# A Fourier filter with a gated convolution: the first batch loaded in 52-row transfers, its first rows sent ahead, and the inverse matrices read from memory

## The chip, the cores and the metric

One Trainium2 chip; the program runs on one of its cores. A core has a matrix engine (TensorE, PE in the profile; PEld is its weight load, which runs beside it), VectorE (DVE), ScalarE (ACT), GpSimd (POOL) and SyncE (SP), which here only issues transfers. Transfers run on 16 DMA engines and are issued from the queues of SP and ACT. PE multiplies out of SBUF (128 partitions) into PSUM; DVE and ACT bring results from PSUM to SBUF. The metric is the time of one launch on the device, in microseconds (us).

## The reference

`x` is 8 batches of 3200 positions with 256 channels. A real Fourier transform along the positions, a complex 256x256 matrix with a bias and a soft threshold on each frequency, the inverse transform; then a gate from a five-tap causal convolution per channel, a value matrix, and an output matrix. Everything is float32.

```python
X = np.fft.rfft(x, axis=1)
Yr = Xr @ w_r - Xi @ w_i + b_r
Yi = Xr @ w_i + Xi @ w_r + b_i
Yr = np.sign(Yr) * np.maximum(np.abs(Yr) - lam, 0.0)      # the same for Yi
x = np.fft.irfft(Y, n=3200, axis=1)
gate = sigmoid(sum(conv_w[k] * shifted(x, k) for k in range(5)))
out = (gate * (x @ w_val)) @ w_out
```

## The kernel before

**The transform in two steps.** 3200 = 50 x 64. A position is n*64 + h*32 + m, with n from 0 to 49, h the half (0 or 1) and m from 0 to 31. Stage 1 (`p1`) transforms over n with the 50x50 matrix `f1`: 50 rows of `x` lie on partitions for each half h (half 1 begins at partition 64), and 50 rows come out, f = 0 to 49, which are the real and imaginary parts of 25 frequency tiles. A batch is cut into 8 units `u` of four m each; one unit is two transfers of 50 rows x 4 KB, four matmuls of 512 columns, a copy out of PSUM, and the stores to a scratch tensor in DRAM, `a_dram`, whose rows are ordered (f, h, m). Stage 2 reads `a_dram` back with the rows on partitions in another arrangement: a frequency tile t is 128 consecutive rows, which come from two values of f. So no tile can be loaded before all 8 units have stored their part of its rows.

**The spectral part** (`p2`) takes two tiles at a time, a pair `u` = 0 to 12 (the last has one tile). Load of `a` (256 KB a pair), stage 2 (`s` in the profile, line 590: f2 matrices), splits into high and low parts on ACT and DVE, the complex matrix in three real products (`k_ps`, line 665, six matmuls; `y_ps`, line 660, twelve), bias, soft threshold (`yb`, `tp`), and, for two pairs at a time, the first inverse stage (`z_ps`, line 703), copied and stored to a second scratch tensor, `z_dram`. The last tile alone ends in line 695, once per batch.

**The last part** (`positions`, `gated`) loads `zl` from `z_dram`, does the second inverse stage (`y_p`, line 759) into `y_sb`, the taps on DVE (line 813), the sigmoid on ACT, the value matmuls `v_ps`, the product with the gate (line 855) and the output matmuls `o_ps` (lines 787 and 791).

**What sets the order.** Nothing is written in engine order. Each piece of work is added to a `Plan` with a priority `at`, an engine, an estimated length, the keys that it reads and writes, and the buffers that it opens. `Plan.order` then plays the program through with these estimates: on each engine, of the pieces that could begin about first, it takes the one with the lowest `at`, and the pieces are emitted in that order. The table `O` shifts the priorities of kinds of work; `SWITCH` is the estimated cost of going between tiled matmuls (mode "q") and others; `WIRE` and `BACKLOG` are a model of the transfers. So a change of any number can move instructions everywhere. Waits on other engines and on transfers are put in by the framework; transfers share eight completion semaphores in turn, so that a queue waits with a ninth until the first has landed.

**The start.** The sixteen transfers of batch 0's `x` go half from SP, half from ACT's queue. PE does warm-up matmuls on a buffer of zeros (line 907) between the units' products (line 508). `f2` is loaded in four parts (pair 0; 1 to 3; 4 to 7; the rest). The matrices of the first inverse stage, `g1`, are the transposes of f2 scaled by 1/64: `make_g1` multiplies f2 with a unit matrix on PE (line 424) and scales on ACT (line 426), pair by pair during batch 0; only the last tile's is loaded. `w_val`, `w_out` and `conv_w` come as float64 words and are converted by 13 operations each on DVE (`from_float64`).

## Time and profile before

| | |
|---|---|
| launch times, 3 runs | 899.44, 899.5 and 904.92 us, median 899.5 |
| span of the profiled execution (first to last instruction) | 897.1 us; the page prints no time of its own for that launch, and the median of the three lies 2.4 us above its span |
| busy: PE, DVE, ACT | 865.2, 763.5, 603.7 us |
| mean granted PE clock | 0.986 |
| data moved | 162.26 MB, 181 GB/s over the span |

In the profile a row of the timeline has start, length, engine, line, operation with output<-input, count, and in brackets the idle time before it with what ended it. In rows of windows each engine has its busy time and, in brackets, its instructions; then the granted PE clock (1.00 is full), the busy share of the 16 DMA engines, and GB/s. PE's float32 matmuls show two records each, so that `x8` of line 590 are four matmuls. Names are without buffer numbers. SPq and ACTq are the engines' issuing of transfers.

### The profile page before, as it was taken

Reading aid. Unit: us, or ns where it says so; the run is one execution under the profiler, and the core shown is the slowest. Engines: PE = TensorE matmul, PEld = TensorE weight load, DVE = VectorE, ACT = ScalarE, POOL = GpSimd, SP = SyncE. Lnnn points to the kernel's source line nnn. Section 1 sums busy time; section 2 is a strip of 40 time slices with the busy share of each in tenths; the row PEclk is TensorE's granted clock in tenths of the full one; section 3 lists DMA queues with packets and bytes.
Section 4 is the critical chain, followed back from the end, with each engine's and each line's share of the span. In section 5 each row is a group of like instructions: output and inputs, shape, how many; then the busy total and the mean of one; then the engine's idle time right before and its main releaser. Section 6 shows DMA issues by size and latency. Waiting matters only on the chain.

```text
span 897.1 us, 24381 instructions
## 1 busy us (share of the span) xinstructions
PE 865.2 (96%) x10370; PEld 741.1 (83%) x10370; DVE 763.5 (85%) x1139; ACT 603.7 (67%) x924; POOL 4.4 (0%) x11
## 2 busy tenths in 40 slices
...
GB/s 203 198 233 239 228 227 217 210 130 182 236 180 179 159 229 218 190 183 160 217 235 158 163 204 217 222 131 174 215 223 154 139 172 109 178 62 116 180 75 91
DMA packets 103439, 162.26 MB, mean 181 GB/s; under 512 B 9154, under 2 KB 77636, under 8 KB 103332
## 3 DMA queue, kind: packets, MB, share of 16 engines
...
## 4 chain that ended last, share of the span: by engine, by line
PE 83%; DVE 10%; DMA 4%; ACT 2%; issue 1%; ACTq 1%; SPq 0%
PE y_ps L660 14%; PE o_ps L791 13%; PE v_ps L791 12%; PE s L590 10%; PE z_ps L703 9%; PE k_ps L665 8%; PE y_p L759 7%; PE p L543 6%; DVE acc L813 4%; DMA x<-in_x 1%; PE v_ps L787 1%; DVE acc L855 1%; DVE gated L317 1%; DMA f_sb<-in_f 1%; DMA a_dram<-s 1%
## 5 line engine op out<-in xcount | busy, mean ns | idle before, releaser
L813 DVE SCALAR_TENSOR_TENSOR acc<-y_sb,cw_sb,acc 128x800 f32<-128x800 f32 (+1 forms) x264 | 255.9, 1018 | 17.6 <-ACT acc L810 17.2
L660 PE MATMUL y_ps<-w_sb,xs 128*128 128x256 f32 x1152 | 155.4, 284 | 0.6 <-DVE xs L648 0.6
L791 PE MATMUL o_ps<-gated,wo_sb 128*128 128x400 f32 x756 | 155.2, 351 | 0.6 <-DVE acc L855 0.6
L660 PEld LDWEIGHTS y_ps<-w_sb,xs 128*128 128x128 f32 x1152 | 144.5, 189 | 11.3 <-DVE xs L652 3.2
L791 PEld LDWEIGHTS o_ps<-gated,wo_sb 128*128 128x128 f32 x756 | 133.5, 188 | 3.1 <-DVE acc L855 0.8
L791 PE MATMUL v_ps<-y_hl,wv_sb 128*128 128x400 f32 x660 | 131.3, 346 | 0.5 <-ACT o L879 0.5
L590 PE MATMUL s<-f_sb,a 128*128 128x128 f32 x800 | 113.2, 284 | 8.2 <-ACT wo_sb L315 3.4
L791 PEld LDWEIGHTS v_ps<-y_hl,wv_sb 128*128 128x128 f32 x660 | 118.5, 188 | 1.6 <-ACT o L879 0.9
L590 PEld LDWEIGHTS s<-f_sb,a 128*128 128x128 f32 x800 | 101.7, 196 | 20.8 <-issue 6.9
L678 ACT ACTIVATE tp<-yb,nlam 128x512 f32<-128x512 f32 (+1 forms) x104 | 73.7, 708 | 38.7 <-DVE yb L674 38.6
L665 PEld LDWEIGHTS k_ps<-w_sb,xs 128*128 128x128 f32 x576 | 77.2, 190 | 20.8 <-issue 10.5
L703 PE MATMUL z_ps<-tp,g_sb 64*64 64x256 f32 x1536 | 93.4, 381 | 0.0
L665 PE MATMUL k_ps<-w_sb,xs 128*128 128x256 f32 x576 | 91.1, 294 | 1.2 <-DVE yb L671 0.9
L759 PEld LDWEIGHTS y_p<-g_sb,zl 50*64 50x64 f32 x4096 | 68.3, 135 | 18.1 <-issue 7.3
L315 ACT CAST gated<-acc 128x800 fp32r<-128x800 f32 x63 | 54.3, 862 | 38.2 <-DVE acc L855 38.0
L759 PE MATMUL y_p<-g_sb,zl 50*64 50x50 f32 x4096 | 72.5, 219 | 7.1 <-issue 4.2
L680 DVE SCALAR_TENSOR_TENSOR tp<-yb,tp 128x512 f32<-128x512 f32 (+1 forms) x104 | 70.0, 673 | 10.6 <-ACT tp L678 10.5
L671 DVE TENSOR_TENSOR yb<-k_ps,bias_sb 128x512 f32<-128x512 f32 x96 | 65.6, 684 | 15.7 <-PE k_ps L665 15.6
L703 PEld LDWEIGHTS z_ps<-tp,g_sb 64*64 64x64 f32 x1536 | 55.3, 133 | 27.4 <-issue 5.1
L855 DVE TENSOR_TENSOR acc<-v_ps,acc 128x800 f32<-128x800 f32 x64 | 62.9, 984 | 16.1 <-PE v_ps L791 12.7
L674 DVE TENSOR_TENSOR yb<-y_ps,yb 128x512 f32<-128x512 f32 x96 | 65.5, 683 | 7.4 <-PE y_ps L660 6.9
L714 ACT COPY z_t<-z_ps 128x1024 f32<-128x1024 f32 x48 | 48.5, 1010 | 25.7 <-PE z_ps L703 25.1
...
## 6 DMA issues: line engine op xcount, KB each, us to landing
zl<-z_dram SPq DMA_DIRECT2D x128, 200.0 KB
...
x<-in_x SPq DMA_DIRECT2D x120, 200.0 KB
a_dram<-s SPq DMA_DIRECT2D x120, 200.0 KB
...
```

What stands on the lines that cost most here:

```text
L590: nc.tensor.matmul(spec()[:, c, :, i, :], tl[ka][:, i, c * P:(c + 1) * P], f2_of(i), start=True, stop=True)
L660: nc.tensor.matmul(p[:, 1 - r, :], xm(hx, c, r), w_sb[:, m, hw, c, :], start=k == 0, stop=k == 5)
L665: nc.tensor.matmul(p, sm(hx, c), w_sb[:, 0, hw, c, :], start=k == 0, stop=k == 5)
L671: nc.vector.tensor_tensor(out=buffer(kb, "yb", [P, 2, D]), in0=tl[kk].rearrange("p (a d) -> p a d", a=1).to_broadcast([P, 2, D]), in1=bias ...
L674: add(at + 0.2, "DVE", dve(2 * D), lambda: nc.vector.tensor_tensor(out=yb(), in0=tl[ky], in1=yb(), op=ALU.add), [ky + (0,)], [kb + (0,)])
L678: nc.scalar.activation(out=buffer(kt, "tp", [P, 2, D])[:, 0:n], in_=tl[kb][:, 0:n], func=AF.Relu, bias=nlam)
L680: add(at + 0.2, "DVE", dve(n * D), lambda: nc.vector.scalar_tensor_tensor(out=tl[kt][:, 0:n], in0=tl[kb][:, 0:n], scalar=LAM, in1=tl[kt][: ...
L703: nc.tensor.matmul(p[e * HP:(e + 1) * HP, i, j * D:(j + 1) * D], g[i * HP:(i + 1) * HP, r, e * HP:(e + 1) * HP], tl[kts[j]][i * HP:(i + 1) ...
L759: nc.tensor.matmul(pv[h][e * HP:(e + 1) * HP, c, m, :], zt[half(h), m, c * P + e * HP:c * P + (e + 1) * HP], g2_sb[half(h), :], start=True ...
L791: nc.tensor.matmul(p[:, e, 0:TB], w[:, hw, c, e * P:(e + 1) * P], src(hy, c), start=n == 0, stop=n == 5)
L813: nc.vector.scalar_tensor_tensor(out=acc(c), in0=y_of(c, j), scalar=cw_sb[:, c, j:j + 1], in1=acc(c), op0=ALU.mult, op1=ALU.add)
L855: add(at + O["gate"], "DVE", dve(2 * TB), lambda: nc.vector.tensor_tensor(out=gate(), in0=hn(tl[kv][:, :, 0:TB]), in1=gate(), op=ALU.mult) ...
```

## The change

**Wider transfers.** `x` is read in 52 rows a half instead of 50 (`NF = N2 + 2`; the two extra rows belong to the next batch and are not multiplied; batch 7 stays at 50), and `a_dram` has 104 rows instead of 100, stored from 52 partitions; rows 50 and 51 of f hold zeros and are read by nobody.

**Batch 0.** Each of the 8 units is its own piece: two transfers (three of the sixteen on ACT's queue, the others on SP's), four matmuls, a copy shared by DVE and ACT. The input lands in the space of `y_sb`, unit 7 in an `x` buffer. Each unit's result is stored in two groups: rows f = 0 to 15 (all that pairs 0 to 3 need) at once, in two transfers of 64 KB, and rows 16 to 51 later, in two of 144 KB. The loads of pairs 0 to 3 wait for the first group alone. The loads of batch 1's `x` come behind pair 3.

**The inverse matrices.** `g1` is computed on the host and loaded in three parts (512, 512 and 576 KB); the transposes, their scalings and the unit matrix are gone. In the first inverse stage one matmul with 64x128 weights takes the place of two with 64x64.

**The order.** The planner now knows the eight semaphores (`LANES`), the supply of PE's instructions in packets (`supplied`), other costs, and table `O` has other values.

```diff
-WARM = 2, 1, 1, 1, 10
+WARM = 6, 1, 1, 1, 1, 1, 1, 1, 8
-SWITCH = {"rq": 97, "fq": 97, "qr": 100, "qf": 100}
-WIRE = 230
-BACKLOG = 5000
+SWITCH = {"rq": 97, "fq": 97, "qr": 170, "qf": 170}
+WIRE = 210
+BACKLOG = 4000
+LANES = 8
+AHEAD, PACKET, TRIGGER, FETCH = 449, 256, 130, 6000
+NF = N2 + 2
+EARLY = 16
 O = {
...
-     'p1': 1.752,
+     'p1': 5.864,
...
-     'conv': 1.176,
+     'conv': 22.106,
...
+    GROUPS = ((0, EARLY), (EARLY, NF))
+    FIRST = [("stored", 0, (u, k, g)) for u in range(8) for k in range(2) for g in range(2)]
+    def p1_loads():
+        src = x.rearrange("b (n h m) c -> h (b n) (m c)", h=NH, m=NM)
+        wide = y_sb.rearrange("p c h n -> p (c h n)")[:, 0:7 * 4 * D]
+        queue = (("SP", nc.sync), ("ACT", nc.scalar))
+        def load(u, h):
+            dst = wide[:, u * 4 * D:(u + 1) * 4 * D] if u < 7 else tl[k7] if h else room(k7, "x", 4 * D)
+            queue[h and u < 3][1].dma_start(out=dst[h * HP:h * HP + NF, :], in_=src[h, 0:NF, u * 4 * D:(u + 1) * 4 * D])
...
+    def p1_store(u, g, at, chain=None):
+        ks, (lo, hi) = ("s1", (0, u)), GROUPS[g]
+        def store(k):
+            if ("a_dram", 0) not in tl:
+                buffer(("a_dram", 0), "a_dram", [NH * NF, NM * D])
+            dst = tl["a_dram", 0].rearrange("(f h) mc -> f h mc", h=NH)
+            st = tl[ks].rearrange("p (h n) -> p h n", h=NH)
+            at_ = u * 4 * D + k * 512
+            nc.sync.dma_start(out=dst[lo:hi, :, at_:at_ + 512], in_=st[k * HP + lo:k * HP + hi])
...
     def p2(b, u, at):
...
+        groups = [None] if b else [0] if 4 * u + 4 <= EARLY else [0, 1]
+        add(at + O["load_a"] * (b > 0 or u > 3) - 4 * (b == 0 and u < 2), "SP", 400, load,
+            [("a_dram", b, j if b else (j, k, g)) for j in range(8) for g in groups for k in range(2 if b == 0 else 1)], [ka + (0,)],
+            {ka: "a"}, kb=80 * n, chain="a" if b or u > 3 else "early")
...
     def load_g1(at, part):
+        t = slice(G1_PARTS[part] * 2 * P, min(G1_PARTS[part + 1] * 2, NT) * P)
+        add(at, "SP", 400, lambda: nc.sync.dma_start(out=g1_sb[:, t], in_=g1[:, t]), STORED, [("g1", part, 0)], kb=(t.stop - t.start) / 3.2)
...
                 for r in range(2):
                     for i in range(2):
-                        for e in range(2):
-                            nc.tensor.matmul(p[e * HP:(e + 1) * HP, i, j * D:(j + 1) * D],
-                                             g[i * HP:(i + 1) * HP, r, e * HP:(e + 1) * HP],
-                                             tl[kts[j]][i * HP:(i + 1) * HP, r, :], start=r == 0, stop=r == 1)
+                        nc.tensor.matmul(p[:, i, j * D:(j + 1) * D], g[i * HP:(i + 1) * HP, r, :],
+                                         tl[kts[j]][i * HP:(i + 1) * HP, r, :], start=r == 0, stop=r == 1)
```

SP's queue at the start of the program, before: `x` the input, `b_sb` the biases, `st` the two complex matrices, `f_sb` f2, `s_128` and so on the results of stage 1.

```order
L496 DMA x<-in_x 50x1024 x8
L432 DMA b_sb<-in_b_r 1x256
L432 DMA b_sb<-in_b_i 1x256
L327 DMA st<-in_w_r 128x2x256
L327 DMA st<-in_w_i 128x2x256
L898 DMA eye_sb<-in_eye 128x128
L411 DMA f_sb<-in_f 128x256
L519 DMA a_dram<-s_128 50x1024 x2
L519 DMA a_dram<-s_154 50x1024 x2
L519 DMA a_dram<-s_174 50x1024 x2
L519 DMA a_dram<-s_198 50x1024 x2
L574 DMA a<-a_dram 128x2x256 x2
```

The same place after, from behind the thirteen loads of `x` on this queue to the first loads of `a`: a store of 32 rows carries 16 values of f and both halves.

```order
L543 DMA a_dram<-s_119 32x1x512 x2
L543 DMA a_dram<-s_128 32x1x512 x2
L543 DMA a_dram<-s_140 32x1x512 x2
L543 DMA a_dram<-s_147 32x1x512 x2
L424 DMA f_sb<-in_f 128x512
L339 DMA st<-in_w_r 128x2x256
L543 DMA a_dram<-s_158 32x1x512 x2
L339 DMA st<-in_w_i 128x2x256
L543 DMA a_dram<-s_169 32x1x512 x2
L543 DMA a_dram<-s_183 32x1x512 x2
L543 DMA a_dram<-s_197 32x1x512 x2
L594 DMA a<-a_dram 128x2x256 x2
```

The first `a` now stands behind 1 MB of stores instead of behind all that batch 0 stores, and f2 for two pairs ahead of it instead of for one. What follows on SP after, up to the loads of pairs 4 to 6 (the three `a` in the last row):

```order
L543 DMA a_dram<-s_128 72x1x512 x2
L594 DMA a<-a_dram 128x2x256
L543 DMA a_dram<-s_140 72x1x512 x2
L543 DMA a_dram<-s_147 72x1x512 x2
L594 DMA a<-a_dram 128x2x256
L543 DMA a_dram<-s_158 72x1x512 x2
L543 DMA a_dram<-s_169 72x1x512 x2
L543 DMA a_dram<-s_183 72x1x512 x2
L543 DMA a_dram<-s_197 72x1x512 x2
L424 DMA f_sb<-in_f 128x1024
L429 DMA g_sb<-in_g 128x1024 x2
L594 DMA a<-a_dram 128x2x256 x3
```

The rest of batch 0's stores, a part of f2 and two parts of g1 now stand between the loads of pair 3 and of pair 4.

PE in the same stretch, before, from its last warm-up matmuls (`s2` is stage 2 and the number its pair's buffer, `p1` stage 1 of batch 1):

```order
L907 MATMUL warm_93<-idle_81 128x512 x10
L590 MATMUL s2_240<-f2_sb_69,a_227 128x2x64 x2
L449 MATMUL bias_2_243<-b_sb_67 128x256 x4
L451 MATMUL bias_1_244<-b_sb_67 128x256 x2
L590 MATMUL s2_240<-f2_sb_69,a_227 128x2x64 x2
L590 MATMUL s2_257<-f2_sb_69,a_229 128x2x64 x4
L543 MATMUL p1_270<-x_231,f1_sb_68 64x512 x4
L543 MATMUL p1_284<-x_237,f1_sb_68 64x512 x4
L665 MATMUL k_ps_296<-w_sb_72,xs_267 128x256 x6
L660 MATMUL y_ps_310<-w_sb_72,xs_267 128x256 x12
```

And after, from pair 2 on:

```order
L612 MATMUL s2_349<-f2_sb_68,a_263 128x2x64 x4
L687 MATMUL k_ps_360<-w_sb_71,xs_346 128x256 x6
L682 MATMUL y_ps_372<-w_sb_71,xs_346 128x256 x12
L687 MATMUL k_ps_402<-w_sb_71,xs_367 128x256 x6
L682 MATMUL y_ps_411<-w_sb_71,xs_367 128x256 x12
L724 MATMUL z_ps_428<-tp_327,g1_sb_70 128x256 x4
L724 MATMUL z_ps_428<-tp_370,g1_sb_70 128x256 x4
L612 MATMUL s2_441<-f2_sb_68,a_388 128x2x64 x4
L612 MATMUL s2_451<-f2_sb_68,a_392 128x2x64 x4
L724 MATMUL z_ps_468<-tp_409,g1_sb_70 128x256 x4
```

Pairs 0 to 3 are mixed before any stage 1 of batch 1, and the first inverse group stands between them and pair 4's stage 2 (`s2_441`); before, stage 1 of batch 1 came right behind pair 1's stage 2.

More of the change, by code (lines that the diff above doesn't have):

```diff
@@ L90, in __init__, with add @@
         self.opened, self.last = {}, {}
-    def add(self, at, engine, busy, fn, uses=(), sets=(), new=None, delay=None, mode="r", kb=0, chain=None, extra=0):
+    def add(self, at, engine, busy, fn, uses=(), sets=(), new=None, delay=None, mode="r", kb=0, chain=None, extra=0, moves=1, ins=0):
         n = len(self.pieces)
@@ L102, in add @@
             self.writers[key], self.readers[key] = [n], []
-        p = dict(n=n, at=at, engine=engine, busy=busy, fn=fn, before=before, new=new or {}, mode=mode, kb=kb, extra=extra,
+        p = dict(n=n, at=round(at, 5), engine=engine, busy=busy, fn=fn, before=before, new=new or {}, mode=mode, kb=kb, extra=extra, moves=moves, ins=ins,
                  tiles={key[:2] for key in (*uses, *sets)}, delay=busy + LAND[engine] if delay is None else delay)
@@ L178, in order @@
                 busy, delay, mode = busy + to, delay + to, p["mode"]
+                while PACKET * len(fetched) + TRIGGER <= ran + p["ins"]:
+                    fetched.append(start + p["busy"] * (PACKET * len(fetched) + TRIGGER - ran) / p["ins"] + FETCH)
+                ran += p["ins"]
             if p["kb"]:
@@ L181, in order @@
                 delay = wire - start + 1400 + p["extra"]
+                landings += [start + delay] * p["moves"]
             free[e] = start + busy
@@ L432, in load @@
                 nc.sync.dma_start(out=b_sb[0:1, k * D:(k + 1) * D], in_=b.rearrange("(o d) -> o d", o=1))
-        add(-91, "SP", 800, load, (), [("b", 0, 0)], kb=20)
+        add(-96.5, "SP", 800, load, (), [("b", 0, 0)], kb=20, moves=2)
         def marks():
@@ new lines, in p1_first @@
+    def p1_first(u, at):
+        kx, kp, ks = ("x", (0, u)), ("p1", (0, u)), ("s1", (0, u))
+        tag = ("s1", "s1", "zst", "zst", "acc", "acc", "g_hl", "g_hl")[u]
+        wide = y_sb.rearrange("p c h n -> p (c h n)")
+        def products():
+            xt, p = wide[:, u * 4 * D:(u + 1) * 4 * D] if u < 7 else tl[kx], two_banks(kp)
+            for h in range(NH):
+                for k in range(2):
+                    nc.tensor.matmul(p[k * HP:(k + 1) * HP, h, :], f1_sb[half(h), :],
+                                     xt[half(h), k * 512:(k + 1) * 512], start=True, stop=True)
+        st = lambda: tl[ks].rearrange("p (h n) -> p h n", h=NH)
+        def keep(h):
+            if h == 0:
+                room(ks, tag, 1024)
+            (nc.scalar.copy if h else nc.vector.tensor_copy)(out=st()[:, h], in_=tl[kp][:, h])
+        add(at, "PE", 890, products, [kx + (h,) for h in range(NH)] + [("f1", 0, 0)], [kp + (0,), ("turn", "p1", u)], {kp: "ps_2"}, mode="q", ins=16)
+        for h, eng in enumerate(("DVE", "ACT")):
+            add(at + 0.01, eng, act(512) if h else dve(512), lambda h=h: keep(h), [kp + (0,)],
+                [ks + (h,)] + ([START[h]] if u == 7 else []), None if h else {ks: tag})
+        p1_store(u, 0, at + 0.02)
@@ L688, in p2 @@
         kts = [("tp", (b, v)) for v in both]
-        gs = [("g1", 2 * v, 0) for v in both]
+        gs = [g1_key(v) for v in both]
         nz = 1 if last else 4
@@ L744, in load @@
                 nc.sync.dma_start(out=zt[half(h)], in_=src[h, :, k * MB:(k + 1) * MB, :])
-        add(at + O["load_z"], "SP", 700, load, [("z_dram", b, u) for u in range(NU)], [kz + (0,)], {kz: "zl"}, kb=400, chain="zl")
+        add(at + O["load_z"], "SP", 700, load, [("z_dram", b, u) for u in range(NU)], [kz + (0,)], {kz: "zl"}, kb=400, chain="zl", moves=2)
         def views():
@@ L896, in begin @@
             nc.sync.dma_start(out=f1_sb[h * HP:h * HP + N2, :], in_=f1)
-    def load_eye():
-        nc.sync.dma_start(out=eye_sb, in_=eye)
-    add(-200, "SP", 800, begin, (), [("f1", 0, 0)], kb=20)
+    add(-200, "SP", 800, begin, (), [("f1", 0, 0)], kb=20, moves=2)
     ki, kw = ("idle", 0), ("warm", 0)
@@ L928, in later_constants @@
                 load_f2(u + 0.1, i)
+        for i, v in ((0, 0), (1, 2), (2, 5)):
+            if u == v:
+                load_g1(u + 0.1, i)
         if u == 7:
```

217 lines of the change are left out of this document (96 added, 121 removed).

## The prediction

> **What bounds the kernel now.** I read the page's head and the chain of waits first, for the engine that sets the end.
>
> ```profile
> span 897.1 us, 24381 instructions
> ...
> PE 865.2 (96%) x10370; PEld 741.1 (83%) x10370; DVE 763.5 (85%) x1139; ACT 603.7 (67%) x924; POOL 4.4 (0%) x11
> ...
> PE 83%; DVE 10%; DMA 4%; ACT 2%; issue 1%; ACTq 1%; SPq 0%
> ```
>
> TensorE (PE) is busy for 96% of the span and carries 83% of the chain. The average hides two regimes, so I asked next for stretches of 50 us (length, busy time of each engine with instruction count, granted clock, DMA share, GB/s).
>
> ```profile
> 0.00:50.00 50.00, 38.88 (x142) 16.81 (x142) 11.32 (x16) 11.09 (x18) 1.14 (x9) 0.83 0.63 200
> 50.00:100.00 50.00, 50.00 (x493) 42.21 (x486) 32.32 (x60) 32.90 (x60) 0.00 (x0) 1.00 0.77 235
> ...
> 150.00:200.00 50.00, 50.00 (x751) 44.57 (x749) 48.04 (x71) 39.98 (x61) 0.00 (x0) 1.00 0.58 188
> ```
>
> From 50 us on PE is full; what happens there can only change by PE work or by order. The first 50 us are different: much of their 38.88 us busy is warm-up matmuls on zeros. So the start is what this change can shorten. Its order of time, from the timeline of the engines and DMA queues:
>
> ```profile
> 1.57 9.82 SPq L496 DMA_DIRECT2D x<-in_x  x8
> ...
> 28.35 9.07 PE L907 MATMUL warm<-idle 128*128 128x512 f32 x20
> ...
> 36.64 0.91 SPq L574 DMA_DIRECT2D a<-a_dram  x2
> ...
> 39.42 0.71 PE L590 MATMUL s<-f_sb,a 128*128 128x128 f32 x4 [1.99 <-DMA a<-a_dram]
> ...
> 45.85 2.05 PE L590 MATMUL s<-f_sb,a 128*128 128x128 f32 x8 [1.65 <-DMA f_sb<-in_f]
> ...
> 119.99 0.59 PE L695 MATMUL z_ps<-tp,g_sb 128*128 128x256 f32 x2
> ```
>
> Stage 2 cannot begin before all of batch 0 has gone to a_dram and come back: 39.42 us for pair 0, 45.85 for pair 1, whose f2 was late. Line 695 closes the spectral part of batch 0 at 119.99; it runs once per batch. I use it as a checkpoint: counting matmuls ahead of it in both orders, the two kernels have done the same work there but for the transposes (line 424, gone) and half a pair of stage 2; so also at the seven later ones.
>
> Transfers fill the start. The 5 us and 20 us stretches:
>
> ```profile
> 5.00:10.00 5.00, 2.53 (x11) 0.93 (x13) 0.00 (x0) 1.28 (x1) 0.00 (x0) 0.85 0.64 201
> 10.00:15.00 5.00, 5.00 (x16) 1.14 (x13) 1.22 (x1) 1.01 (x1) 0.00 (x0) 0.50 0.67 254
> ...
> 20.00:25.00 5.00, 1.87 (x11) 0.61 (x11) 1.22 (x1) 1.01 (x1) 0.00 (x0) 1.00 0.63 222
> 25.00:30.00 5.00, 5.00 (x24) 2.32 (x17) 2.72 (x4) 2.42 (x4) 0.00 (x0) 0.66 0.63 235
> ...
> 60.00:80.00 20.00, 20.00 (x205) 17.11 (x204) 13.35 (x24) 13.47 (x24) 0.00 (x0) 1.00 0.82 279
> 100.00:120.00 20.00, 18.27 (x180) 13.16 (x180) 17.36 (x47) 11.59 (x21) 0.00 (x0) 1.00 0.79 241
> ```
>
> While only 50-row transfers run, the DMA share stands at 0.63 to 0.67 with 201 to 254 GB/s; with mixed transfers it reaches 0.82 and 279.
>
> The Trainium skill (DMA: Bandwidth & Descriptors, in the section on why a DMA increments its semaphore by 16) says that a transfer runs on the largest number of engines up to 16 that divides its outer sizes. By that rule 50 rows get 10 engines and 52 rows 13; 10 of 16 is 0.625, so the trace agrees, and the first loads would end about 2 us before my figure below.
>
> **The first 46 us.** I price transfers of the changed kernel at 279 GB/s, the one long stretch with mixed sizes; 235 (the 50 to 100 us stretch) is the low end, and the high end is 254 GB/s at 0.67 raised to the share of 0.82, 311. Sizes follow from the shapes in the new order.
>
> The loads start at 2 us as before. Sixteen of 208 KB are 3.41 MB: 12.2 us, to 14.2. Then come the 16 early stores of 64 KB, f2 and the two weights, 1.83 MB: 6.6 us, to 20.8. Before, the DMA share fell to almost nothing about 2.2 us before the first load of `a` was issued:
>
> ```profile
> 34.00:36.00 2.00, 2.00 (x6) 0.80 (x6) 0.00 (x0) 0.00 (x0) 0.00 (x0) 1.00 0.16 61
> ...
> 46.00:48.00 2.00, 2.00 (x12) 1.77 (x16) 0.15 (x1) 0.07 (x1) 0.00 (x0) 0.50 0.69 176
> ```
>
> With the same 2.2 us the first `a` is issued at 23.0 and, with 2.8 us to the matmul as before (36.64 to 39.42), stage 2 begins at 25.8 instead of 39.42. What queues ahead of pair 4 on SP is then 5.51 MB: five loads of `a`, two pieces of f2, 16 stores of the remaining rows (144 KB each), and 1 MB of g1 that was not loaded before. That is 19.7 us, and with 0.9 us to land pair 4's rows are there at 43.6. In between PE has pairs 0 to 3. Its prices are start to start, from the timeline of PE:
>
> ```profile
> 71.22 1.09 PE L543 MATMUL p<-x,f_sb 50*64 50x512 f32 x8
> 72.13 1.91 PE L703 MATMUL z_ps<-tp,g_sb 64*64 64x256 f32 x32
> 73.97 0.97 PE L665 MATMUL k_ps<-w_sb,xs 128*128 128x256 f32 x6
> 74.78 1.57 PE L660 MATMUL y_ps<-w_sb,xs 128*128 128x256 f32 x12
> 76.18 0.61 PE L424 MATMUL turned<-eye_sb,f_sb 128*128 128x128 f32 x4
> 76.63 1.06 PE L590 MATMUL s<-f_sb,a 128*128 128x128 f32 x8
> 77.44 0.95 PE L665 MATMUL k_ps<-w_sb,xs 128*128 128x256 f32 x6
> ```
>
> So p costs 0.91, z 1.84, k 0.81, y 1.40, a transpose 0.45, s 0.81 us. Four pairs of s, k and y and one z are 4 x 3.02 + 1.84 = 13.9 us, which fits between 25.8 and 43.6 with 4 us over, though the second z waits for g1. The clock is on my side of neither kernel: in 46 to 48 us it stood at 0.50 after a wait of PE. The Trainium skill (TensorE: Matmul & The Clock Gate, on what is actually happening) puts the fall to half clock at an idle window of about 3.4 us; by it the two waits of the new start would cost up to 1.7 us each if PE, and not the DMA, set the pace there. I take nothing for it, since the 4 us cover it; without them it is those few microseconds.
>
> **From pair 4 to the checkpoint.** The new order has 34.0 us of PE work there up to pair 11 (s 7.0, z 3, p 8, k 7, y 7 times the prices above). SP moves 11.73 MB in the same stretch: 16 x and 12 store pieces of 208 KB, z, `a`, f2, g1, w_val. At 279 GB/s that is 42.0 us: here the DMA, not PE, sets the pace, and 8 us of the lead are given back. Pair 11 is there at 43.6 + 42.0 = 85.6. What is left to the checkpoint is 16.6 us of PE work, and PE idled 1.7 us in 100 to 120 before (18.27 busy of 20), which I keep: 85.6 + 16.6 + 1.7 = 103.9 instead of 120.0. That is **-16.1 us**; the 12 transposes are in it. At 235 GB/s the same sum gives 119.0 (-1.0), at 311 it gives 95.7 (-24.3).
>
> **The rest of the program.** Waits of PE over the whole span, by who ended them:
>
> ```profile
> PE y_p L759 <- issue: 4.2, 4, 1.5
> ...
> PE s L590 <- ACT wo_sb L315: 3.4, 1, 3.4
> ```
>
> The 3.4 us stood behind the conversion of w_out on VectorE and ScalarE, which sat between stage 2 of batch 1 and its mixing. In the new order that conversion (11 rows of DVE and a subtraction) comes while PE has z, two p and two and a half s. I take -3.0, between -3.4 and 0. The "issue" waits stand ahead of the shortest matmuls; the inverse stage's instruction count halves, which can only ease them, while y_p itself is unchanged: -2.1, half, with bounds -4.2 and 0. The new order enters tiled matmuls from others 102 times, before 96, and splits s in 12 places more; k after p costs no more than k after y, so some tenths each: +1.0, bounds 0 and 3.
>
> **The inverse stage.** Sixteen matmuls with 64x64 weights per group become eight with 64x128. From the groups by line:
>
> ```profile
> L590 PEld LDWEIGHTS s<-f_sb,a 128*128 128x128 f32 x800 | 101.7, 196 | 20.8 <-issue 6.9
> ...
> L703 PE MATMUL z_ps<-tp,g_sb 64*64 64x256 f32 x1536 | 93.4, 381 | 0.0
> ...
> L703 PEld LDWEIGHTS z_ps<-tp,g_sb 64*64 64x64 f32 x1536 | 55.3, 133 | 27.4 <-issue 5.1
> ```
>
> 32 records in 1.84 us, each 381 ns: a quarter array each, and four abreast. With 64x128 weights there are 16 records, two abreast, and a weight load of up to 196 ns instead of 133 but half as many. Both give the same 1.84 us; 0 is my value. No row shows this shape. The bounds are 0 and one abreast, 3.68 us, so +88 us in 48 groups; I take the near end, since s hides its 128-column loads at 0.81 us for eight.
>
> ACT loses 12 scalings and the first stores its queue; none is on the path after 50 us, so nothing. Stores of x in 52 rows for 50 add 4% of bytes, already in the sizes above; later the share is 0.58 and covers it.
>
> **Sum.** -16.1 - 3.0 - 2.1 + 1.0 = -20.2 on the span, 876.9 us. The times shown have a median 2.4 us above the span of the profiled execution, so 879.
>
> **Rivals.**
>
> *The transfers of batch 0 become the bound.* For it: 1.6 MB of g1 are added just where the share was 0.82; the new order issues the batch-1 loads later. Against: wider transfers need less share per byte. At 235 GB/s the checkpoint gives 1.0 and the sum 5.1: 894.
>
> *Everything runs faster still.* At 311 GB/s, with both waits gone and the switches free: -24.3 - 3.4 - 4.2, 868. For it speaks that the rate per share was higher at 10 to 15 us than at 60 to 80.
>
> *The order in the middle is worse.* VectorE is busy 48.04 of 50 us there; the new order puts filter taps and splits later against the mixing. If PE waits for DVE's gate by 1.5 us more in each 50 us of 690, that is 21 us: the gain is gone at 1.46 us, and the time is about 900. Against it: the same table of work between checkpoints, and PE full today.
>
> *Slower: the two row halves of the inverse stage don't overlap,* or their weight loads show. Place: line 724 of the changed kernel, 48 groups. It decides from 20.2 / 48 = 0.42 us per group on (2.26 instead of 1.84); at full price 967. Against it: p and z already run row halves abreast.
>
> *It does not do what it says:* the early loads wait for the late stores after all, and stage 2 starts near 39 us. Then the 12 transposes (12 x 0.45 = 5.4 us) and the terms of the rest (4.1) are all that is left: 890.
>
> **Chances.** Forecast (872 to 889) 0.54; faster still 0.15; transfers 0.14; order 0.09; inverse stage 0.05; nothing 0.03. About 1%, 9 us, is what a measurement can tell from no change. Below 890.5 lie the first two, the last and a third of the transfers' case: 0.76. Within 1%: the rest of that and most of the order's: 0.16. Slower: 0.08. For 8 in 10 the range takes in the faster case and the transfers' one: 867 to 896.
>
> **What would show it.** First stage-2 matmul near 26 us and pair 4's near 44; line 717 (the checkpoint) near 104; z groups of 1.84 us; a DMA share above 0.8 from 45 to 85 us; eight checkpoints with the same spacing as before (100 to 103 us); w_out without a wait of PE. A checkpoint at 104 with 890 at the end would make the terms behind it wrong; one at 115 or later, the transfer rate.

## The result, and the profile after

The changed kernel takes 916.1 us (median of 4 runs, 912.7 to 917.5) against 901.0 us for the kernel before on the same chip (899.4 to 904.9). The ratio is 1.016, with a 95% interval of 1.013 to 1.020: **slower by 1.6%**, where 879 us, 2.3% faster, was forecast. The page of the profiled execution, its head and the chain by engine:

```profile
span 910.9 us, 22760 instructions
...
PE 877.5 (96%) x9566; PEld 750.5 (82%) x9566; DVE 765.5 (84%) x1143; ACT 605.6 (66%) x916; POOL 4.2 (0%) x11
...
PE 73%; DVE 15%; DMA 4%; ACT 4%; issue 2%; SPq 2%; ACTq 0%; DVEq 0%
```

The span grew by 13.8 us, from 897.1. PE is still busy 96%, with 12.3 us more of busy time though the transposes are gone, and DVE's share of the chain went from 10% to 15%. The checkpoints (line 717, once per batch) say where the time went. At the eighth, the same numbers of matmuls of every kind have been issued in both kernels; at the first, all but half a pair of stage 2.

| us | before | after | difference |
|---|---|---|---|
| first checkpoint | 119.99 | 121.92 | +1.9 (forecast -16.1) |
| from the first to the eighth | 701.9 | 707.1 | +5.2 (forecast -4.1) |
| eighth checkpoint to the end of the span | 75.2 | 81.9 | +6.7 (forecast 0) |

The start, in order of time, from the timelines of SyncE's queue (SPq) and PE after:

```profile
24.55 3.75 SPq L543 DMA_DIRECT2D a_dram<-s  x6
25.45 10.55 PE L925 MATMUL warm<-idle 128*128 128x512 f32 x20
30.17 0.89 SPq L594 DMA_DIRECT2D a<-a_dram  x2
31.61 3.31 SPq L543 DMA_DIRECT2D a_dram<-s  x4
35.55 3.19 SPq L543 DMA_DIRECT2D a_dram<-s  x4
35.84 1.95 PE L612 MATMUL s<-f_sb,a 128*128 128x128 f32 x16
39.65 6.41 SPq L543 DMA_DIRECT2D a_dram<-s  x8
53.15 3.46 PE L724 MATMUL z_ps<-tp,g_sb 64*128 64x256 f32 x16 [2.03 <-DMA g_sb<-in_g]
56.54 2.23 PE L612 MATMUL s<-f_sb,a 128*128 128x128 f32 x16
...
97.23 2.35 PE L612 MATMUL s<-f_sb,a 128*128 128x128 f32 x12
...
121.92 0.38 PE L717 MATMUL z_ps<-tp,g_sb 128*128 128x256 f32 x1
```

Stage 2 starts at 35.84 instead of the forecast 25.8, pair 4 (the matmuls at 56.54) instead of at 43.6, pair 11 (97.23) instead of at 85.6. The sixteen stores of the later rows cost SP 3.31 + 3.19 + 6.41 = 12.9 us of issuing, 0.81 each, in front of g1 and of the rows that pair 4 needs. That pair 4 is late by the same 12.9 us is chance. 10.0 of them are there when stage 2 begins, which is the moment at which the warm-up matmuls (25.45, 10.55 us long) end; from then to 51.1 us PE works on pairs 0 to 3 with 1.8 us of waits, and only then does it wait 2.03 us, for g1. The windows of the same stretch (length, busy times, granted clock, DMA share, GB/s):

```profile
5.00:10.00 5.00, 5.00 (x21) 1.99 (x23) 0.00 (x0) 0.00 (x0) 0.00 (x0) 1.00 0.85 186
15.00:20.00 5.00, 5.00 (x29) 1.31 (x22) 1.70 (x3) 1.17 (x2) 0.00 (x0) 1.00 0.90 226
20.00:25.00 5.00, 5.00 (x23) 2.53 (x22) 1.06 (x2) 1.17 (x2) 0.00 (x0) 1.00 0.65 171
25.00:30.00 5.00, 5.00 (x10) 2.12 (x9) 3.83 (x6) 3.13 (x6) 0.00 (x0) 0.66 0.57 135
...
45.00:85.00 40.00, 37.34 (x277) 28.29 (x275) 23.58 (x45) 20.47 (x36) 0.00 (x0) 0.96 0.91 297
...
97.00:122.00 25.00, 22.00 (x147) 16.06 (x146) 20.48 (x51) 13.84 (x23) 0.00 (x0) 0.86 0.86 266
```

The first 30 us move 135 to 226 GB/s where I had put 279; from 45 to 85 us the rate is 297. In the last 25 us ahead of the checkpoint PE has 22.0 us of 25 busy, at a granted clock of 0.86. The longest waits of PE over the whole span after (total, times, longest):

```profile
PE y_p L779 <- DVE acc L875: 5.0, 2, 4.8
PE y_p L779 <- ACT s L568: 2.5, 2, 2.0
PE y_p L779 <- issue: 2.2, 4, 1.0
PE s L612 <- ACT xs L673: 2.1, 1, 2.1
PE z_ps L724 <- DMA g_sb<-in_g: 2.0, 1, 2.0
```

The wait of 3.4 us for w_out that the kernel before has in batch 1 is not in this list, and half of the "issue" waits are gone. The longest wait is new; it stands behind the last checkpoint.

### The profile page after: what moved, and what is told of

Read it like the earlier page. It is cut to its first block, busy times and chain, and to the rows that moved or that the text cites. A ratio compares the mean times of both kernels' runs of the same rounds, so it can differ in the third digit from the quotient of the medians.

```text
span 910.9 us, 22760 instructions
## 1 busy us (share of the span) xinstructions
PE 877.5 (96%) x9566; PEld 750.5 (82%) x9566; DVE 765.5 (84%) x1143; ACT 605.6 (66%) x916; POOL 4.2 (0%) x11
## 4 chain that ended last, share of the span: by engine, by line
PE 73%; DVE 15%; DMA 4%; ACT 4%; issue 2%; SPq 2%; ACTq 0%; DVEq 0%
PE o_ps L811 12%; PE y_ps L682 12%; PE v_ps L811 10%; PE z_ps L724 8%; PE s L612 8%; PE k_ps L687 7%; PE y_p L779 6%; DVE acc L833 6%; PE p L563 5%; DMA a_dram<-s 3%; PE v_ps L807 2%; DVE acc L875 2%; SPq L543 1%; PE warm L925 1%; DVE gated L329 1%
## 5 line engine op out<-in xcount | busy, mean ns | idle before, releaser
L833 DVE SCALAR_TENSOR_TENSOR acc<-y_sb,cw_sb,acc 128x800 f32<-128x800 f32 (+1 forms) x264 | 263.0, 1022 | 15.1 <-ACT acc L830 14.6
L811 PEld LDWEIGHTS o_ps<-gated,wo_sb 128*128 128x128 f32 x756 | 135.5, 189 | 7.3 <-DVE gated L329 1.6
L811 PE MATMUL v_ps<-y_hl,wv_sb 128*128 128x400 f32 x660 | 134.4, 349 | 1.4 <-ACT s L568 1.4
L811 PEld LDWEIGHTS v_ps<-y_hl,wv_sb 128*128 128x128 f32 x660 | 116.4, 188 | 2.3 <-ACT s L568 1.6
L724 PE MATMUL z_ps<-tp,g_sb 64*128 64x256 f32 x768 | 98.5, 396 | 4.4 <-DMA g_sb<-in_g 2.0
L724 PEld LDWEIGHTS z_ps<-tp,g_sb 64*128 64x128 f32 x768 | 71.7, 190 | 20.1 <-issue 4.1
L702 DVE SCALAR_TENSOR_TENSOR tp<-yb,tp 128x512 f32<-128x512 f32 (+1 forms) x104 | 68.9, 663 | 16.1 <-ACT tp L700 15.6
L669 DVE TENSOR_TENSOR sx<-s,sx 128x256 f32<-128x256 f32 x96 | 40.3, 420 | 39.1 <-ACT xs L666 29.9
L568 ACT COPY s<-p 128x1024 f32<-128x1024 f32 x56 | 56.6, 1013 | 19.2 <-DMA a_dram<-s 10.7
```

What stands on the lines that cost most here:

```text
L568: nc.scalar.copy(out=st, in_=tl[kp])
L702: add(at + 0.2, "DVE", dve(n * D), lambda: nc.vector.scalar_tensor_tensor(out=tl[kt][:, 0:n], in0=tl[kb][:, 0:n], scalar=LAM, in1=tl[kt][: ...
L724: nc.tensor.matmul(p[:, i, j * D:(j + 1) * D], g[i * HP:(i + 1) * HP, r, :], tl[kts[j]][i * HP:(i + 1) * HP, r, :], start=r == 0, stop=r == 1)
L811: nc.tensor.matmul(p[:, e, 0:TB], w[:, hw, c, e * P:(e + 1) * P], src(hy, c), start=n == 0, stop=n == 5)
L833: nc.vector.scalar_tensor_tensor(out=acc(c), in0=y_of(c, j), scalar=cw_sb[:, c, j:j + 1], in1=acc(c), op0=ALU.mult, op1=ALU.add)
```

## The experiments

Each was run beside the kernel before. The columns: first and eighth checkpoint, the stretch behind the eighth, the span (all from one profiled execution of each kernel), and the ratio of the times to the kernel before with its 95% interval.

| kernel | first | eighth | behind | span | ratio |
|---|---|---|---|---|---|
| before | 119.99 | 821.91 | 75.2 | 897.1 | 1 |
| after | 121.92 | 829.02 | 81.9 | 910.9 | 1.016 (1.013 to 1.020) |
| a_oldtable | 118.40 | 824.38 | 85.7 | 910.1 | 1.011 (1.005 to 1.016) |
| b_neworder | 128.32 | 829.29 | 81.5 | 910.8 | 1.010 (1.005 to 1.015) |
| a_64x64 | 122.24 | 823.12 | 84.0 | 907.1 | 1.005 (1.002 to 1.008) |
| b_64x128 | 123.03 | 830.77 | 76.5 | 907.3 | 1.010 (1.005 to 1.016) |
| a_split | 128.44 | 843.26 | 82.2 | 925.5 | 1.024 (1.018 to 1.030) |
| a_pool | 122.61 | 827.44 | 83.6 | 911.0 | 1.014 (1.009 to 1.020) |
| a_warm | 124.36 | 831.06 | 88.1 | 919.2 | 1.022 (1.018 to 1.026) |
| a_onegroup | 121.52 | 834.14 | 83.3 | 917.4 | 1.014 (1.009 to 1.020) |
| a_50 | 123.59 | 833.71 | 81.8 | 915.5 | 1.022 (1.017 to 1.027) |
| a_pool_later | 113.38 | 822.96 | 83.1 | 906.1 | 1.007 (1.003 to 1.011) |
| a_pool_later_64 | 112.61 | 818.44 | 83.9 | 902.3 | 0.998 (0.995 to 1.002) |
| a_pool_later_64_oldplan | 112.49 | 827.38 | 82.1 | 909.5 | 1.010 (1.007 to 1.013) |
| b_newtable | 123.56 | 825.22 | 83.9 | 909.1 | 1.015 (1.008 to 1.022) |
| b_newrules | 119.88 | 823.74 | 85.1 | 908.8 | 1.008 (1.004 to 1.011) |
| a_best | 110.77 | 816.77 | 81.4 | 898.2 | 0.997 (0.993 to 1.000) |

One execution is a rough measure: the profiled one of the changed kernel was the fastest of its four, that of a_64x64 the slowest of its ten (903.5 to 908.9 us). Behind the eighth checkpoint the changed kernel, a_50, a_split, a_onegroup, a_pool and a_pool_later have the same number of matmuls and the same longest wait, and take 81.8 to 83.6 us. So differences of 1 or 2 us in the columns of checkpoints show nothing; the ratio has all runs in it.

My theory from the two traces: the start is held by SP's issuing of the later rows; the middle and the end by the new order. The rivals: bytes in flight for the start, the 64x128 inverse stage for the middle.

### The inverse stage: a_64x64 and b_64x128

```diff
-                        nc.tensor.matmul(p[:, i, j * D:(j + 1) * D], g[i * HP:(i + 1) * HP, r, :],
-                                         tl[kts[j]][i * HP:(i + 1) * HP, r, :], start=r == 0, stop=r == 1)
+                        for e in range(2):
+                            nc.tensor.matmul(p[e * HP:(e + 1) * HP, i, j * D:(j + 1) * D],
+                                             g[i * HP:(i + 1) * HP, r, e * HP:(e + 1) * HP],
+                                             tl[kts[j]][i * HP:(i + 1) * HP, r, :], start=r == 0, stop=r == 1)
```

This is a_64x64; b_64x128 is the same edit backwards in the kernel before.

> The changed kernel with the inverse stage in 64x64 quarters as before (16 matmuls and 16 weight loads a group instead of 8). If the wide form costs what the starts show, 1.93 us a group instead of 1.84, 48 groups give back 4.3 us: 911 to 913. If the engine has room for it, or the order that the planner makes of it decides, 916 within 2 us.

> The kernel before with only the inverse stage of the change: eight matmuls with 64x128 weights a group instead of sixteen with 64x64. The other way round the narrow form gave 6.2 us between the first and the last checkpoint (707.1 to 700.9, 42 groups, 0.15 us each). If that is the form itself, the kernel before gets slower by 6 to 7.5 us, 906 to 909, and its checkpoints are 707 to 709 apart instead of 701.9. If it was the order that the planner made around it (the planner counts the same price for both), the time stays within 2 us of before.

With the narrow form the changed kernel reaches its eighth checkpoint at 823.1 instead of 829.0, and the ratio falls from 1.016 to 1.005, by more than the 4.3 us that I had expected. With the wide form the kernel before, in the same order, needs 707.7 us from its first checkpoint to the eighth instead of 701.9, +5.8 (its first checkpoint is late by 3.0 besides; its waits of PE for rows of `a` are 5.6 us instead of 2.0, which the form doesn't explain). So the middle's loss is the inverse stage, and my theory of the order falls there. The timeline of PE shows how. The kernel before, groups followed by a tiled `p` and by an untiled `k_ps`:

```profile
220.72 1.96 PE L703 MATMUL z_ps<-tp,g_sb 64*64 64x256 f32 x32
222.49 1.04 PE L543 MATMUL p<-x,f_sb 50*64 50x512 f32 x8
...
238.10 1.96 PE L703 MATMUL z_ps<-tp,g_sb 64*64 64x256 f32 x32
239.98 0.97 PE L665 MATMUL k_ps<-w_sb,xs 128*128 128x256 f32 x6
```

The same two places in b_64x128:

```profile
222.93 2.00 PE L702 MATMUL z_ps<-tp,g_sb 64*128 64x256 f32 x16
224.86 1.09 PE L543 MATMUL p<-x,f_sb 50*64 50x512 f32 x8
...
240.51 2.00 PE L702 MATMUL z_ps<-tp,g_sb 64*128 64x256 f32 x16
242.44 0.97 PE L665 MATMUL k_ps<-w_sb,xs 128*128 128x256 f32 x6
```

Start to start, ahead of `k_ps` the wide group costs 1.93 instead of 1.88 us; ahead of `p` 1.93 instead of 1.77. All groups between the checkpoints that the timeline shows whole, with another kind of matmul next and no wait in between, say the same: before, 29 with `p` or `y_p` next cost 1.73 to 1.78 and 8 with an untiled matmul next 1.88 or 1.89; in b_64x128 all 40 cost 1.92 or 1.93. So the narrow form is cheaper where `p` or `y_p`, which use tiles of 64 columns too, come next, and the planner puts most groups there. 42 groups times 0.16 are 6.7 us if all stood so; the two experiments show 6.2 (707.1 to 700.9) and 5.8. That a change of tile shape is the reason is read from these rows; it was not tried apart from the weight loads, which change with it. The Trainium skill (TensorEngine Tiling (Array Packing), under the key properties of the tiling modes) states that changing the tiling mode drains TensorE. The rows agree: 64x64 is cheap where 64-column tiles follow (1.77 us), and 64x128 costs the same before either (1.93).

### The first rows: a_50, a_warm, a_onegroup

```diff
-            queue[h and u < 3][1].dma_start(out=dst[h * HP:h * HP + NF, :], in_=src[h, 0:NF, u * 4 * D:(u + 1) * 4 * D])
+            queue[h and u < 3][1].dma_start(out=dst[h * HP:h * HP + N2, :], in_=src[h, 0:N2, u * 4 * D:(u + 1) * 4 * D])
```

(a_50, with the same in the later loads and stores.)

> The changed kernel with 50 rows instead of 52 in all loads of x, and in the stage-1 stores of batches 1 to 7. If the wider transfers carry more bytes per us, as I forecast, the first loads end 2 to 4 us later and the time rises by 2 to 4 us, to 918 to 920. If they only keep more engines busy with the same bytes (0.85 share at 186 GB/s against 0.64 at 201 in the same stretch of before), the first loads end no later and the time is within 3 us of 916, or below.

Windows of a_50, to be set against those after:

```profile
5.00:10.00 5.00, 5.00 (x17) 1.98 (x19) 0.00 (x0) 0.00 (x0) 0.00 (x0) 1.00 0.65 184
15.00:20.00 5.00, 5.00 (x29) 1.05 (x25) 1.38 (x2) 1.39 (x3) 0.00 (x0) 1.00 0.74 229
```

184 and 229 GB/s at a share of 0.65 and 0.74, where 52 rows moved 186 and 226 at 0.85 and 0.90. The wider form keeps more engines busy and moves no more bytes per us. The start of stage 2 (36.29 instead of 35.84) can't show when the rows came, since in both runs it is the end of the warm-up matmuls; SP's queue can: a_50 issues its first load of `a` at 29.25 us, the changed kernel at 30.17, so the narrow loads were no later. The total, 1.022, is on the side of my forecast, but the intervals overlap and what it lost lies behind the first loads (710.1 instead of 707.1 us between the checkpoints), so the later batches are left open.

```diff
-WARM = 6, 1, 1, 1, 1, 1, 1, 1, 8
+WARM = 6, 1, 1, 1, 1, 1, 1, 1, 2
```

> The changed kernel with 2 idle matmuls instead of 8 behind the last unit of the start. If these (10.55 us on a slow clock) are what stage 2 waits for, it starts at 31 to 34 instead of 35.84. If the rows of a are only there by then, it starts at 35 to 36 behind a wait for that transfer, on a lower clock, and nothing is gained. Either way the loads of pair 4 are not touched: pair 4 stays at 55 to 57 and the time within 3 us of 916.

```profile
26.30 3.70 PE L925 MATMUL warm<-idle 128*128 128x512 f32 x8
32.90 2.02 PE L612 MATMUL s<-f_sb,a 128*128 128x128 f32 x16 [2.90 <-DMA a<-a_dram]
...
52.21 3.47 PE L724 MATMUL z_ps<-tp,g_sb 64*128 64x256 f32 x16 [2.68 <-DMA g_sb<-in_g]
```

PE of a_warm: the rows of `a` are there at 32.9, so the warm-up held stage 2 for 2.9 us. Pair 4 gains little by it and starts at 55.61, because the first inverse group now waits 2.68 us for g1. The time of 1.022, outside the 3 us that I had allowed, is not the price of the warm-up alone: behind the eighth checkpoint this kernel has 775 matmul records instead of 750, so the planner put the later batches in another order too.

```diff
-    GROUPS = ((0, EARLY), (EARLY, NF))
+    GROUPS = ((0, NF),)
```

(a_onegroup; the second round of stores goes, and pairs 0 to 3 wait for the whole rows.)

> The changed kernel with the rows of batch 0 stored in one piece per half unit (16 stores of 52 rows' worth, 208 KB) instead of 16 rows ahead and 36 behind, so that the second row of sixteen issues goes. If the split costs more issue time than it gains, the first stage 2 is later (37 to 41 instead of 35.8) but pair 4 is earlier (48 to 53 instead of 56.5), the checkpoint is at 112 to 118, and the time is 905 to 912. If the split does what I forecast of it, the checkpoint is later than 122 and the time over 918.

```profile
20.00:25.00 5.00, 5.00 (x24) 2.39 (x21) 1.38 (x2) 1.17 (x2) 0.00 (x0) 1.00 0.93 346
```

That window of a_onegroup stands against 0.65 and 171 after. Stores of 52 rows keep the engines full, at 346 GB/s, where those of 16 rows, 0.62 us of issuing for 64 KB (3.75 us for six), left them at a share of 0.57 to 0.65. The first load of `a` is issued at 33.29 instead of 30.17: so to send a third of the rows ahead gained 3.1 us on the queue. Stage 2 shows only 0.5 of it (36.35), because the warm-up matmuls hold it in both. Pair 4 starts near 50, as expected for this case, but the first checkpoint, forecast at 112 to 118, stays at 121.5. So did that of a_pool, below.

### The queue of the later rows: a_split, a_pool

```diff
-            nc.sync.dma_start(out=dst[lo:hi, :, at_:at_ + 512], in_=st[k * HP + lo:k * HP + hi])
+            (nc.gpsimd if g else nc.sync).dma_start(out=dst[lo:hi, :, at_:at_ + 512], in_=st[k * HP + lo:k * HP + hi])
```

(a_pool; a_split has ScalarE for every other store of the second group.)

> The changed kernel with every other one of the sixteen second-group stores issued by ScalarE instead of SyncE. If SyncE's issue time (16 times 0.81 us, 12.9 us) is what holds the loads for pair 4 back, half of it goes: pair 4 starts near 50 instead of 56.5, the first checkpoint is near 116 instead of 122, and the time is 909 to 912. If the bytes in flight set the pace, pair 4 stays within 2 us of 56.5 and the time within 2 us of 916.

> The changed kernel with all sixteen second-group stores issued by GpSimd, which has nothing else to do there, instead of SyncE. If SyncE's issue time (16 times 0.81 us, 12.9 us) is what keeps the loads for pair 4 back, they are issued some 12 us sooner: pair 4 starts at 44 to 47 instead of 56.5, the first checkpoint at 108 to 113 instead of 122, and the time is 902 to 908. If the bytes in flight set the pace, pair 4 stays within 2 us of 56.5. If the wait only moves to a later transfer, pair 4 comes early and the checkpoint stays within 3 us of 122.

a_split failed for its own reason. ScalarE of a_split, its queue (ACTq) and the copy behind it:

```profile
33.73 5.12 ACTq L543 DMA_DIRECT2D a_dram<-s  x4
38.89 0.37 ACT L662 COPY sx<-s 128x256 f32<-128x256 f32 x1 [8.86 <-DMA a_dram<-s]
```

Four issues took 5.12 us (waits for a free semaphore may be in it), in front of the copies that PE waits for; pair 4 stays at 56.69. With the stores on GpSimd pair 4 starts at 52.28 instead of 56.54, so SP's issuing was worth 4.3 us of its start, less than the 9.5 to 12.5 expected: the wait for g1 and the slow group behind it are gone, and what is left between stage 2's start at 36.22 and pair 4 is PE's work on pairs 0 to 3, with one wait of 1.16 us. The checkpoint did not move at all (122.61). PE and DVE of a_pool, further on:

```profile
85.38 2.14 DVE L368 TENSOR_SCALAR st<-st 128x512 int32<-128x512 int32 x5
...
94.84 0.42 DVE L674 TENSOR_TENSOR xs<-sx,xs 128x256 fp32r<-128x256 f32 x1
95.31 1.22 PE L687 MATMUL k_ps<-w_sb,xs 128*128 128x256 f32 x4 [6.03 <-DVE xs L674]
96.46 3.79 PE L724 MATMUL z_ps<-tp,g_sb 64*128 64x256 f32 x16
```

From 85.38 to 94.84 DVE converts w_val and conv_w, and the split that PE needs (line 674) stands behind all of it: 6.03 us of waiting, and then a group at half clock, 3.79 us instead of 2.00. The same happens to w_out from 106 to 113 us, with 3.3 us of waiting. These waits ate what the stores on GpSimd had gained.

The changed kernel itself has smaller ones at the same two conversions (DVE, ACT and PE):

```profile
91.57 2.14 DVE L368 TENSOR_SCALAR st<-st 128x512 int32<-128x512 int32 x5
...
102.35 1.13 PE L724 MATMUL z_ps<-tp,g_sb 64*128 64x256 f32 x8 [0.84 <-DVE tp L702]
...
109.94 2.15 DVE L368 TENSOR_SCALAR st<-st 128x512 int32<-128x512 int32 x5
...
116.63 0.41 DVE L669 TENSOR_TENSOR sx<-s,sx 128x256 f32<-128x256 f32 x1
...
117.27 0.40 ACT L673 CAST xs<-sx 128x256 fp32r<-128x256 f32 x1
...
117.75 0.68 PE L612 MATMUL s<-f_sb,a 128*128 128x128 f32 x4 [2.07 <-ACT xs L673]
118.19 2.75 PE L682 MATMUL y_ps<-w_sb,xs 128*128 128x256 f32 x12
```

DVE converts w_val and conv_w from 91.57 to 101.1 and w_out from 109.94 to 116.6. Behind the first PE waits 0.84 us, behind the second 2.07, and from 118.2 to 120.9 it has a granted clock of 0.53.

### The conversions: a_pool_later

```diff
-     'later': -9.891,
+     'later': 4.406,
```

> The changed kernel with the second-group stores on GpSimd, and with the table's 'later' back from -9.891 to 4.406, so that the conversions of w_val, conv_w and w_out (8.5 us and 7.5 us of VectorE in one stretch) no longer stand ahead of the splits that PE waits for. If these conversions swallowed the lead of 4.3 us that pair 4 had with the stores on GpSimd (waits of PE for VectorE of 6.0 and 3.3 us, and a slow clock behind each), the first checkpoint comes at 110 to 115 instead of 122.6 and the time is 902 to 907. If PE then waits for loads of x and of a instead, the checkpoint stays at 119 to 124 and the time at 911 to 915.

The first checkpoint is at 113.38, as forecast. But only the wait for w_out is gone, whose conversion now lies between other work of DVE. The last part of that of w_val and conv_w (91.8 to 97.5 us) still stands ahead of a pair's splits, and PE waits there, in two parts and 4.9 us in all instead of 6.0:

```profile
96.19 0.50 PE L682 MATMUL y_ps<-w_sb,xs 128*128 128x256 f32 x2 [3.06 <-ACT xs L666]
...
98.49 2.50 PE L682 MATMUL y_ps<-w_sb,xs 128*128 128x256 f32 x10 [1.79 <-DVE xs L670]
```

Nor is all of the 9.2 us gain: a unit of `p`, two pairs of `k_ps` and one of `y_ps` that a_pool issued ahead of it now come behind, 0.91 + 1.62 + 1.40 = 3.9 us at the prices of the prediction. At the eighth checkpoint, with equal work, it is 4.5 us ahead of a_pool, and the span is 4.9 us shorter.

### The order: a_oldtable, b_neworder, b_newtable, b_newrules

```diff
-     'gate': 0.469,
+     'gate': -3.751,
```

(One line of many: a_oldtable is the changed kernel with the whole table O of before. b_neworder is the kernel before with the new table and the new rules of the planner, b_newtable and b_newrules with one of them.)

> The changed kernel with the table O of the kernel before (the planner's rules and constants stay the new ones). If the new table is what costs the 8.9 us that the checkpoints show between the second and the sixth batch (-0.6 us against before at the second, +8.2 at the fifth, +9.0 at the sixth) and the 6.7 us behind the last one (81.9 instead of 75.2), the time falls from 916 to about 901 to 904, and the distance of the checkpoints in the middle is 101 to 103.5 again. If these losses belong to the 64x128 inverse stage or to the 52 rows, the time stays within 3 us of 916.

> The kernel before with the new table O, the new constants and the new rules of the planner, with the same loads, stores, transposes and inverse stage as before. If the new order is the cause in the middle and at the end, the time rises from 900 to about 912 to 916, with 81 to 82 us behind the last checkpoint. If the 64x128 inverse stage or the 52 rows are the cause, it stays at 897 to 903.

> The kernel before with the new table O alone; planner's rules and constants stay the old ones. If the table costs the 6 to 7 us behind the last checkpoint, that stretch is 80 to 83 us (75.2 before; 81.5 with table and rules) and the time is 905 to 909. If the rules cost it, the stretch is 74 to 77 us.

> The kernel before with the planner's new rules and constants alone; the table O stays the old one. If the rules cost the stretch behind the last checkpoint, it is 80 to 83 us and the time is 905 to 909. If the table costs it, the stretch is 74 to 77 us. If neither alone does, both are near 75, and only the pair is to blame.

The old table in the new kernel gains 4.6 us up to the eighth checkpoint and loses 3.8 behind it (12 matmuls of `o_ps`, about 1.1 us, moved from the one to the other); it missed 901 to 904 because neither the end came back nor the middle (706.0 us between the checkpoints instead of 701.9). The new order on the old kernel costs 1.0%: 8.3 us at the first checkpoint (four units of `p` more stand ahead of it, 3.6 us), nothing between the checkpoints (701.0), and 6.3 at the end. At the end either part alone is enough to lengthen it: 83.9 us with the new table alone (with 12 matmuls of `v_ps` more, about 1.1 us), 85.1 with the new rules alone, 75.2 with the old pair, 76.5 with the old pair and the wide inverse stage.

### Together: a_pool_later_64, a_pool_later_64_oldplan, a_best

```diff
+O_LAST = {**O, **{k: v for k, v in {'y': 0.522, 'conv': 1.176, 'val': 2.74, 'gate': -3.751, 'project': 5.91, 'p3': 3.595, 'load_z': -3.135}.items() if k in ('y', 'conv', 'val', 'gate', 'project', 'p3', 'load_z')}}
...
-        add(at + O["gate"], "DVE", dve(2 * TB), lambda: nc.vector.tensor_tensor(
+        add(at + O_of(b)["gate"], "DVE", dve(2 * TB), lambda: nc.vector.tensor_tensor(
```

(a_best: a_pool_later_64 with the old values for these keys in the last batch alone.)

> The three corrections at once: stores on GpSimd, 'later' at 4.406, inverse stage in 64x64. If they add up, the first checkpoint is at 110 to 115, the next seven steps take 701, and with the 82 to 84 us of the new order at the end the sum is 893 to 900, as fast as the kernel before or a little faster. If the lead of the start is given back in batch 1, the first two checkpoints are no earlier than before (211.6) and the time is 903 to 908.

> The same three corrections and the planner's rules and constants of the kernel before (mode switch 100, no limit of transfers under way, no instruction supply, the old prices of bytes). If the new rules cost the 6.7 us behind the last checkpoint (81.9 after, 81.5 with the new order on the old kernel, 75.2 before), the stretch behind the last checkpoint is 75 to 78 us and the time is 6 us below the kernel with the three corrections. If the table does, it stays at 81 to 85.

> The three corrections (stores on GpSimd, 'later' at 4.406, inverse stage in 64x64), and in the last batch alone the old values of the table for the positions, the taps, the gate and the two projections. If these values cost the end (PE waits 4.8 us once for the gate on VectorE), the stretch behind the last checkpoint goes from 83.9 to 76 to 79, and the time is 893 to 897, below before. If the order of the batches ahead of it costs the end, it stays at 82 to 85 and the time at 900.

The three corrections add up: 5.9 us (inverse stage) and 4.7 us (from a_64x64 to a_pool_later_64 at the eighth checkpoint) bring the ratio from 1.016 to 0.998. The old rules make it worse again, 1.010, and leave the end at 82.1. The old values in the last batch bring the end from 83.9 to 81.4, not to 76 to 79, and the best ratio, 0.997 with an interval of 0.993 to 1.000: at most a little faster than the kernel before. The time, 896.3 us, lies in the 893 to 897 that I had expected, but not for the reason given. The wait of 4.8 us for the gate did go (the longest wait of PE there is now 1.5 us); other, shorter waits came, and PE's waits behind the eighth checkpoint fell only from 9.3 to 8.0 us in sum.

## Why the prediction was wrong

The sum was -20.2 on the span and +13.8 came: 34.0 us. 18.0 of them lie ahead of the first checkpoint, 9.3 between the checkpoints, 6.7 behind.

**The first 46 us: failed, by 12.9 us at pair 4.** "I price transfers of the changed kernel at 279 GB/s" is the step. The loads of `x` ran at 186 to 226 GB/s, and the windows of the early stores, f2 and the weights at 135 to 171. The 3.41 + 1.83 MB of the sum, from 2 us to the last early store's issue at 28.3, are 199 GB/s; with that rate the sum's own steps put the first load of `a` at 30.5, and it was issued at 30.17 instead of the forecast 23.0. The rows of the same stretch before, which the prediction shows, gave 201 to 254. A rate taken from a stretch with many transfers under way was put on a stretch that had short ones. That their issue on SP, 0.62 us for each early store, is why the rate was low is not shown: SP also waited 7.7 us up to 30 us for loads of `x` to land before it could issue the next transfer, and no run changes one of the two alone. From that load to stage 2 it was 5.7 us instead of 2.8, of which a_warm shows 2.9 to be the warm-up. These two make the 10.0 us by which stage 2 was late. The other 2.9 came behind it: the wait for g1 and the slow group after it, which the later stores' issuing (0.81 us each) caused; to move them to GpSimd brought 4.3 us. The rule of the Trainium skill cited there (DMA: Bandwidth & Descriptors, on why a DMA increments its semaphore by 16) fits the shares, 0.85 with 52 rows against 0.65 with 50. What I drew from it, loads that end 2 us earlier, is refuted by a_50: the bytes per us are the same.

**From pair 4 to pair 11: right in its length, not in its reason.** 42.0 us were forecast and 40.7 measured (56.54 to 97.23), at 297 GB/s in 45 to 85 us. But the forecast had PE wait for the DMA for 8 of them, and PE does not:

```profile
56.54:97.23 40.69, 39.44 (x296) 28.38 (x294) 26.64 (x51) 23.62 (x39) 0.00 (x0) 1.00 0.87 272
```

It is busy 39.4 of 40.7 us, with 0.7 us of recorded waits for a load. The matmuls are those that I had counted, so it was their 34.0 us that came out too short, and that the two agree is luck. Part of the excess may be loads of `x` that hold a unit of `p` in its middle (two of the eight took 1.9 and 2.2 us instead of 1.1); the rest is not explained.

**From pair 11 to the checkpoint: failed, by 6.4 us** (24.7 instead of 16.6 + 1.7). The order of DVE was looked at for w_out's sake alone: "that conversion comes while PE has z, two p and two and a half s". PE does have those. But the 7 us of w_out now come on top of the 9.5 of w_val and conv_w, ahead of the splits of batch 0's last pairs, and I never asked who else waits on DVE there. The changed kernel waits 0.84 and 2.07 us behind the two and has a granted clock of 0.86 in the stretch. That the conversions are the cause is shown with the stores on GpSimd (a_pool against a_pool_later), where the waits are larger; with the stores on SP it is read from the rows.

**The rest of the program.** Of -2.1 for the "issue" waits, 2.0 came (4.2 to 2.2 on `y_p`). The 3.4 us wait for w_out is gone from batch 1, but the wait of 2.07 us at 117.75 stands behind the same conversion, now ahead of the first checkpoint, so little of the -3.0 was gained. And without the inverse stage the stretch between the checkpoints gained 1.0 us (700.9 in a_64x64 against 701.9), not 4.1.

**The inverse stage: failed, 0 against +5.9.** The price of 1.84 came from a group that was followed by an untiled matmul, and there it holds within 0.1 (1.93). Most groups stand ahead of `p` or `y_p`, where the narrow form cost 1.77. Nor does the row say "four abreast": 32 records of 381 ns are 12.2 us, 6.6 times 1.84. My rival for it had the place right but the wrong mechanism (overlap and weight loads) and a far larger price, 0.42 us from which it decides.

**The end: not in the sum at all.** DVE of the kernel after in the last batch, then PE:

```profile
852.56 9.96 DVE L833 SCALAR_TENSOR_TENSOR acc<-y_sb,cw_sb,acc 128x800 f32<-128x800 f32 x10 [5.56 <-ACT acc L830]
862.44 0.98 DVE L875 TENSOR_TENSOR acc<-v_ps,acc 128x800 f32<-128x800 f32 x1
...
863.48 2.82 PE L779 MATMUL y_p<-g_sb,zl 50*64 50x50 f32 x96 [4.84 <-DVE acc L875]
```

DVE idles 5.56 us, begins its taps 23.5 us behind the checkpoint, does ten at a stretch, and only then the gate that PE waits for, 4.84 us. Before, the taps began 17.2 us behind:

```profile
839.12 2.02 DVE L813 SCALAR_TENSOR_TENSOR acc<-y_sb,cw_sb,acc 128x800 f32<-128x800 f32 x2 [2.25 <-ACT acc L810]
```

"Order in the middle is worse" named this wait, for DVE's gate, but put it into every 50 us of the middle. It is in the last batch, where there is no other batch's work to fill PE. But it is not the whole 6.7 us: a_best removes it and gets back 2.5. Behind the eighth checkpoint all waits of PE together are 9.2 us after against 5.1 before, and the same 750 matmul records keep PE busy 69.4 us at a granted clock of 0.95, before 66.7 at 0.99. Which of the waits brings the lower clock with it, and why every other order of the last batch that was tried has an end of 81 us or more, stays open.

**The rivals and the signs.** "Transfers become the bound" is refuted for the middle (297 GB/s), and a rate below its 235 came in the first 30 us, where it had not looked. "It does not do what it says" came near in its number for stage 2 (39; measured 35.84). The sign I had given for a checkpoint at 115 or later, the transfer rate, is half right: it was that rate in the first 30 us, the warm-up, the issuing, and DVE. Of the other signs the DMA share came (0.91 from 45 to 85 us), the price of z did not (1.93). The spacing of the checkpoints before is not 100 to 103 us but 91.6 to 106.5; after, it is 89.1 to 107.9.
